# LSH attention with two feed-forward layers: first token block placed between the steps of the second batch's attention, one planned order for all engines, values unsplit, gate as one function

## Chip, cores and metric

One Trainium2 chip, one core. The time is the device time of one execution in microseconds (us), as a median over several runs. Engines: PE (TensorE: matmuls and transposes), DVE (VectorE), ACT (ScalarE), POOL (GpSimd), SP (issues DMAs).

## The reference, cut to what matters

```python
# q, k, v: (2 batches, 8 heads, 768 tokens, 64); proj: (64, 6); all matmul inputs f32 or f64
q_bucket = sum(((q @ proj) > 0) * powers); k_bucket = sum(((k @ proj) > 0) * powers)
scores = where(q_bucket[:, None] == k_bucket[None, :], q @ k.T / 8, -1e9)
attn = exp(scores - max); attn = attn / (sum(attn) + 1e-9)
x = (attn @ v) of all heads side by side             # (1536 tokens, 512)
h = x @ w_in                                         # (1536, 2048), w_in f64
x = (h * tanh(log1p(exp(min(h, 20))))) @ w_out       # (1536, 512)
out = (((x @ w1) * (x @ w2)) @ w3) @ w_out2          # widths 1024, 1024, 1024, 512
```

The f64 weights arrive as pairs of 32-bit words.

## The kernel before, in words

**Split numbers.** For f32 accuracy an operand is written as hi + lo, both in the format f32r, which the PE takes in one pass. A product is then three matmuls (`PASS`: hi·hi, hi·lo, lo·hi). A split is one ACT copy (hi) and one subtraction (lo) on DVE or POOL (`split`, L175 to 178).

**Weights.** A chunk of 128 x 1024 f64 numbers is loaded as 32-bit words (`load64`, 1 MB, L128), decoded to f32 by one ACT and three DVE passes (`decode_a`, `decode_b`: L136, L139, L162, L166), stored in DRAM as f32 for the two later token blocks (`keep`, L277), and split (L176, L177). There are 36 such chunks: 4 of `w_out2`, 8 of `w3`, 8 of `w_in`, 8 of `w_out`, 4 of `w1`, 4 of `w2`. The product `w3 @ w_out2` is made once (`wp_mm`, L806, 192 matmuls of 512 columns) and kept in DRAM as `wp`.

**Attention.** 16 heads of 6 row tiles are 96 steps. A step computes the scores of 128 queries against 768 keys (`scores`, four matmuls of 384 columns, L638), the maximum on DVE (L648), and the exponential with its sum on ACT (L652). Later each 128 x 384 piece of the exponentials is transposed on the PE (`t_step`, three transposes, L693), copied out as hi by ACT (L710) and lo by DVE (L711), and multiplied with the values (`av_step`, L729: two matmuls of 384 columns, one for hi and one for lo; V's hi and lo stand side by side in the 128 columns of the stationary operand). Each step has two such pieces. The four partial products of a head leave by ACT (L740) and go through DRAM (`x_d`, L745; row sums r through `r_d`; means of V through `mv_d`), because hi and lo halves and the two heads of a pair lie in different partitions. `x_split` (L351 to L365) reads them back and makes the split input of a token block. Before a head's scores, its queries and keys are split, transposed (`qk_transpose`, L560) and given bucket bits (`bits`, L590 to L615); the features and masks are moved between partitions by DMA (`qa<-qb`, `qa<-mk` and others).

**Feed-forward.** The 1536 tokens are three blocks of 512. A block is 672 matmuls of 512 columns: 192 for h (`h_mm`, L380), 192 for its output (`out_mm`, L1011), 192 for the two products with w1 and w2 (`ab_mm`, L1038), 96 for the last one (`o_mm`, L1062). The gate (`mish`, L414 to L424) is four DVE passes (one of them on POOL in some chunks) and three ACT functions (Exp, Ln, Exp) over 128 x 1024.

**Order.** `PLAN` at the top of the file says by hand at which attention step each piece of other work is traced (`tail`, `filler`, `prep`); Tile's scheduler orders by that. The attention runs alone with the weight product; of the first token block only three h chunks (72 matmuls) are traced among the last attention steps (`e0` to `e5`). The rest of the block follows the attention, then the second and third block (list `prog`). All DMAs but one are issued from SP. The lines of the hand-written order that the change removes are

```python
tl("xs", lambda: x_split(0))
tl("e0", lambda: h_early(0, 0, 0))
tl("m0", lambda: mish(0, 0))
segs = dict(s=seg_s, p=seg_p, n=seg_n, t=seg_t, f=seg_f, l=seg_l)
for c in PLAN["ord"]:
    segs[c]()
```

Of the kernel before, what the change touches and what calls it, by code (L numbers as in the profile page):

```python
# [8 lines left out]
PLAN = {'sp': [],  # L9
 'F32N': 0,  # L10
 'F32E': 1000,
 'GPM': [4, 5, 6],
 'GPL': [4],
 'wg': [2, 2, 2, 2],
 'kw': [0, 4, 0, 0, 0, 2],
 'pe1': 0,
 'ord': 'nsptlf',
 'sg': [203, 204],
 'bx': 1,
 'wo2n': [0, 3, 0, 3],  # L20
# [46 lines left out]
PSUM = bass.MemoryType.PSUM  # L67

# [4 lines left out]
DRAM = bass.MemoryType.DRAM  # L73
TINY = float(2.0 ** -80)
SIGN = -(2 ** 31)


@with_exitstack
def kernel(
# [22 lines left out]
    NP = NH // 2  # L102
# [3 lines left out]
    KR = D + 2 * NB  # L106

    const = ctx.enter_context(tc.tile_pool(name="const", bufs=1))
    big = ctx.enter_context(tc.tile_pool(name="big", bufs=2))
    strm = ctx.enter_context(tc.tile_pool(name="strm", bufs=2))  # L110
    ps = ctx.enter_context(tc.tile_pool(name="ps", bufs=1, space=PSUM))

    def ps_s(name, dt=F32):
        return ps.tile([128, 2, 512], dt, tag="s", name=name, bufs=2)

    dram = ctx.enter_context(tc.tile_pool(name="dram", bufs=1, space=DRAM))
    x_d = [dram.tile([DM, NT], F32, tag=f"x{i}", name=f"x_d{i}") for i in range(2)]
    r_d = dram.tile([2, DM // 128, NT], F32, tag="r", name="r_d")
    mv_d = [dram.tile([2, DM], F32, tag=f"mv{i}", name=f"mv_d{i}") for i in range(B)]
    wp_d = dram.tile([FF2, DM], F32, tag="wp", name="wp_d")  # L120
    ident = const.tile([128, 128], F32, tag="ident", name="ident")
    identr = const.tile([128, 128], FR, tag="identr", name="identr")

    c04 = const.tile([128, 1], F32, tag="c04", name="c04")

    def load64(src, n, pool=strm):
        raw = pool.tile([128, n, 1024 // n, 2], I32, tag="raw", name="raw", bufs=2)
        nc.sync.dma_start(out=raw.rearrange("p a b t -> p a (b t)"), in_=src)  # L128
        return raw, pool

    def decode_a(raw):
        raw, pool = raw
        n = raw.shape[1]
        g = pool.tile([128, n, 1024 // n], F32, tag="g", name="g", bufs=2)
        z = raw[:, :, :, 1]
        nc.scalar.activation(  # L136
            out=g, in_=raw[:, :, :, 1].bitcast(F32), func=AF.Copy, scale=2.0 ** -112
        )
        nc.vector.tensor_scalar(  # L139
            out=z, in0=g.bitcast(I32), scalar1=3, scalar2=None, op0=ALU.logical_shift_left  # L140
        )
        return raw, g, z

    def decode_b(state, sg=False):
        raw, g, z = state
        if sg:
            sg = min(sg, 2)
            nc.vector.scalar_tensor_tensor(
                out=z, in0=raw[:, :, :, 0], scalar=29, in1=z,
                op0=ALU.logical_shift_right, op1=ALU.bitwise_or,  # L150
            )
            if sg == 2:
                nc.gpsimd.tensor_scalar(
                    out=g, in0=g, scalar1=0.0, scalar2=2.0, op0=ALU.is_ge, op1=ALU.mult
                )
                nc.gpsimd.tensor_mul(out=g, in0=z.bitcast(F32), in1=g)
                nc.gpsimd.tensor_sub(out=g, in0=g, in1=z.bitcast(F32))
                return g
            nc.scalar.activation(out=g, in_=g, func=AF.Sign)
            nc.gpsimd.tensor_mul(out=g, in0=z.bitcast(F32), in1=g)  # L160
            return g
        nc.vector.scalar_tensor_tensor(  # L162
            out=z, in0=raw[:, :, :, 0], scalar=29, in1=z,
            op0=ALU.logical_shift_right, op1=ALU.bitwise_or,
        )
        nc.vector.scalar_tensor_tensor(  # L166
            out=g.bitcast(I32), in0=g.bitcast(I32), scalar=SIGN, in1=z,
            op0=ALU.bitwise_and, op1=ALU.bitwise_or,
        )
        return g  # L170

    def decode(raw, sg=False):
        return decode_b(decode_a(raw), sg)

    def split(src, n, hl, eng):  # L175
        nc.scalar.copy(out=hl[:, 0], in_=src)  # L176
        eng.tensor_sub(out=hl[:, 1], in0=src, in1=hl[:, 0])  # L177
        return hl

    PASS = ((0, 0), (0, 1), (1, 0))  # L180

    # ------------------------------------------------ loads of the feed-forward parts
    TB = 512
    NBK = NT // TB
    FP = FF // 256
    AP_ = FF2 // 256

    SB, HB = 2, 5
    late = []
    mid = []  # L190
    spare = []
    keep = {}
    chunks = {}
    order = []
    prog = []
    HL = PLAN["lookh"]
    for n in range(NBK):
        c = PLAN["cut"] if n + 1 < NBK else None
        nxt = []
        if c:  # L200
            for x in range(HL):
                nxt.append((c[x], [("h", n + 1, x), ("mish", n + 1, x), ("ms", n + 1, x)][:3 if x == 0 else 1]))

        def after(k):
            for kk, ops in nxt:
                if kk == k:
                    prog.extend(ops)

        for j in range(FP):
            if j + HL < FP and (n, j) != (0, 0):  # L210
                prog.append(("h", n, j + HL))
            elif n == 0 and j == 0:
                for x in range(3, HL + 1):
                    prog.append(("h", n, x))
            if j + 1 < FP:
                if (n, j) != (0, 0):
                    prog.append(("mish", n, j + 1))
                prog.append(("ms", n, j + 1))
            if n + 1 < NBK and j == (PLAN["xs1"] if n == 0 else PLAN["xs2"]):
                prog.append(("x", n + 1))  # L220
            prog.append(("out", n, j))
            after(j)
        prog.append(("x2", n))
        after(8)
        prog.append(("ab", n, 0))
        for f in range(FF2 // 128):
            if f + 1 < FF2 // 128:
                prog.append(("ab", n, f + 1))
            after(9 + f)
            prog.append(("o", n, f))  # L230
        after(17)
        prog.append(("fin", n))
    for j in range(3):
        order.append((0, "wi", j))
    order.append((0, "wo", 0))
    for op in prog:
        keys = {
            "h": lambda n, j: [(n, "wi", j)], "out": lambda n, j: [(n, "wo", j)],
            "ab": lambda n, f: [(n, "wa", f // 2), (n, "wb", f // 2)],
            "o": lambda n, f: [(n, "wp", f // 2)],  # L240
        }.get(op[0], lambda *a: [])(*op[1:])
        order.extend(x for x in keys if x not in order)
    issued = [0]

    loaded = {}
    decoded = {}
    nxt_ = [0, 0]

    def load_chunk(i):
        n, nm, j = order[i]  # L250
        pool = strm if i < 8 or i % 4 > 1 or nm in ("wa", "wb") else late[0]
        m = KD if nm in ("wi", "wa", "wb") else 2
        if n == 0 and nm != "wp":
            w = {"wi": w_in, "wo": w_out, "wa": w1, "wb": w2}[nm]
            if m == KD:
                src = w[:, j * 512:(j + 1) * 512].rearrange("(k p) f -> p k f", p=128)
            else:
                src = w[j * 256:(j + 1) * 256].rearrange("(f p) d -> p f d", p=128)
            loaded[i] = load64(src, m, pool)
        else:  # L260
            f = pool.tile([128, m, 1024 // m], F32, tag="g", name="f", bufs=2)
            if nm == "wp":
                nc.sync.dma_start(
                    out=f, in_=wp_d[j * 256:(j + 1) * 256].rearrange("(f p) d -> p f d", p=128)
                )
            else:
                nc.sync.dma_start(out=f.rearrange("p a b -> p (a b)"), in_=keep[nm, j])
            loaded[i] = f

    def decode_chunk(i):  # L270
        n, nm, j = order[i]
        f = loaded.pop(i)
        if n == 0 and nm != "wp":
# [7 lines left out]
    def load_to(i):  # L281
        while nxt_[0] < min(i, len(order)):
            load_chunk(nxt_[0])
            nxt_[0] += 1
# [344 lines left out]
    E = {}  # L629
# [512 lines left out]
```

## Time and profile before

| what | value |
|---|---|
| median of 3 runs | 942.21 us (939.95 to 947.37) |
| span of the profiled execution | 967.6 us |
| PE busy | 822.8 us, 85% of the span |
| DVE busy | 667.6 us, 69% |
| ACT busy | 512.5 us, 53% |
| POOL busy | 203.4 us, 21% |
| DMA | 125.99 MB, 69545 packets, 23152 of them under 512 B |

The profiled execution is one execution of its own; its span is 25.4 us above the median of the runs. PE's busy time is a union of intervals that include each matmul's latency, so a price of a matmul is better read from the distance of two starts than from its duration.

### The profile page before, as it was taken

How to read it: one execution, taken by the hardware profiler on the slowest of the kernel's cores; microseconds unless marked ns; L12 is line 12 of the kernel's file. 1: busy time of each engine (PE TensorE's matmuls, PEld its weight loads, DVE VectorE, ACT ScalarE, POOL GpSimd, SP SyncE). 2: the span in 40 equal slices, each digit the busy share in tenths (PEclk: the TensorE clock that was granted, in tenths of full speed). 3: DMA queues.
4: the chain of work that ended last, by engine and by line, in shares of the span. 5: the costliest groups of instructions: out<-in, count | busy, mean ns of one | idle time of the engine just before them, and what ended most of it. 6: DMA issues, size and time to landing. Idle time of an engine off the chain costs nothing. (4 is left out here: it accounts for less than half of the span.)

```text
span 967.6 us, 11292 instructions
## 1 busy us (share of the span) xinstructions
PE 822.8 (85%) x3923; PEld 686.2 (71%) x3923; DVE 667.6 (69%) x823; ACT 512.5 (53%) x801; POOL 203.4 (21%) x219
## 2 busy tenths in 40 slices
PE   7767987867889666889767398989999999999998
PEld 6656876756777656767545276768888888888886
DVE  6866865754878657877879999975775744766422
ACT  3745774644658364775555456335664633665321
POOL 3240320130203113122275743440000000000000
PEclk8799899988999797989979698989999999999999
DMA  6686798665596855648764566644233233332101
GB/s 203 182 147 134 126 145 152 121 128 102 125 101 83 179 79 111 104 118 100 249 233 159 168 217 214 220 152 150 89 95 102 88 87 108 131 109 88 44 22 44
DMA packets 69545, 125.99 MB, mean 130 GB/s; under 512 B 23152, under 2 KB 33648, under 8 KB 68464
## 3 DMA queue, kind: packets, MB, share of 16 engines
q1 hardware_dynamic: 69344, 125.14, 54.0%
q8 instruction: 31, 0.51, 0.2%
q14 instruction: 26, 0.21, 0.1%
q10 hardware_dynamic: 144, 0.13, 0.0%
HBM read 88.09 MB, written 24.17 MB: 116 GB/s over the span
## 5 line engine op out<-in xcount | busy, mean ns | idle before, releaser
L1011 PE MATMUL x2a<-ghl,hl 128*128 128x512 f32 x552 | 135.9, 403 | 33.3 <-ACT ghl L430 20.4
L1011 PEld LDWEIGHTS x2a<-ghl,hl 128*128 128x128 f32 x552 | 106.4, 194 | 60.6 <-ACT ghl L430 22.2
L729 PE MATMUL pv<-ethl,hlv 128*128 128x384 f32 (+1 forms) x384 | 131.5, 410 | 13.7 <-POOL ethl L709 10.1
L380 PE MATMUL hps<-xhl,hl 128*128 128x512 f32 x552 | 138.4, 401 | 3.9 <-POOL hl L177 3.9
L710 ACT CAST ethl<-et 128x384 fp32r<-128x384 f32 x192 | 90.9, 483 | 92.6 <-PE et L693 83.0
L1038 PE MATMUL abp<-x2hl,hl 128*128 128x512 f32 x576 | 137.2, 394 | 0.0
L711 DVE TENSOR_TENSOR ethl<-et,ethl 128x384 fp32r<-128x384 f32 x192 | 102.9, 551 | 38.9 <-ACT ethl L710 36.9
L1038 PEld LDWEIGHTS abp<-x2hl,hl 128*128 128x128 f32 x576 | 108.1, 188 | 25.8
L380 PEld LDWEIGHTS hps<-xhl,hl 128*128 128x128 f32 x552 | 106.0, 193 | 27.7 <-POOL hl L177 4.3
L693 PE MATMUL et<-ident,E 128*128 128x128 f32 x576 | 106.8, 295 | 21.4 <-DVE ethl L711 21.1
L648 DVE TENSOR_REDUCE st<-ts 128x1 f32<-128x768 f32 x96 | 91.1, 949 | 30.0 <-PE ts L638 29.4
L693 PEld LDWEIGHTS et<-ident,E 128*128 128x128 f32 x576 | 78.4, 152 | 36.2 <-DVE ethl L711 26.8
L652 ACT ACTIVATE E<-ts,st 128x768 f32<-128x768 f32 x96 | 87.4, 911 | 15.3 <-DVE st L648 14.0
L177 DVE TENSOR_TENSOR hl<-f,hl 128x1024 fp32r<-128x1024 f32 x56 | 71.9, 1283 | 32.4 <-ACT hl L176 32.3
L1062 PE MATMUL oac<-hl,phl 128*128 128x512 f32 x288 | 77.2, 420 | 10.3 <-ACT phl L1049 7.1
L729 PEld LDWEIGHTS pv<-ethl,hlv 128*128 128x128 f32 x384 | 68.2, 209 | 18.4 <-POOL ethl L709 10.9
L1062 PEld LDWEIGHTS oac<-hl,phl 128*128 128x128 f32 x288 | 57.9, 203 | 26.3 <-ACT phl L1049 7.9
L638 PE MATMUL ts<-ka,qa 76*128 76x384 f32 x192 | 58.6, 386 | 21.0 <-DMA qa<-mk 12.4
L176 ACT CAST hl<-f 128x1024 fp32r<-128x1024 f32 x60 | 62.9, 1048 | 25.6 <-PE x2a L1011 12.1
L177 POOL TENSOR_TENSOR hl<-g,hl 128x1024 fp32r<-128x1024 f32 x17 | 55.5, 3264 | 61.9 <-ACT hl L176 61.8
L162 DVE SCALAR_TENSOR_TENSOR raw<-raw 128x1024 int32<-128x1024 int32 x34 | 62.0, 1824 | 0.3
L638 PEld LDWEIGHTS ts<-ka,qa 76*128 76x128 f32 x192 | 38.7, 215 | 29.5 <-DMA qa<-mk 10.3
(120 smaller groups left out, 1193.7 us busy)
## 6 DMA issues: line engine op xcount, KB each, us to landing
raw<-in_moe_w_dram SPq DMA_DIRECT2D x16, 1024.0 KB
raw<-in_moe_w_out_dram SPq DMA_DIRECT2D x12, 1024.0 KB
raw<-in_moe_w_in_dram SPq DMA_DIRECT2D x8, 1024.0 KB
f<-keep_wi SPq DMA_DIRECT2D x16, 512.0 KB
f<-keep_wo SPq DMA_DIRECT2D x16, 512.0 KB
x_d<-ptmp SPq DMA_DIRECT2D x64, 96.0 KB
xi<-x_d SPq DMA_DIRECT2D x24, 256.0 KB
f<-wp_d SPq DMA_DIRECT2D x12, 512.0 KB
```

The lines of the kernel that those rows point to most:

```text
L177: eng.tensor_sub(out=hl[:, 1], in0=src, in1=hl[:, 0])
L380: nc.tensor.matmul(o, lhsT=w[:, ws, kk, f * 128:(f + 1) * 128], rhs=xh[xs][:, kk, :], start=(m == 0), stop=(m == 3 * KD - 1),)
L638: nc.tensor.matmul(t[:, a, 0:HS], lhsT=l[0:kk, i * 128:(i + 1) * 128], rhs=r[0:kk, a * HS:(a + 1) * HS], start=(l is qa), stop=(l is qb),)
L648: nc.vector.tensor_reduce(out=s[:, 0, i:i + 1], in_=t[:, :, 0:HS], axis=AX.XY, op=ALU.max, negate=True)
L652: nc.scalar.activation(out=e.rearrange("p (a n) -> p a n", a=2), in_=t[:, :, 0:HS], func=AF.Exp, bias=s[:, 0, i:i + 1], accum_out=s[:, 1, ...
L693: nc.tensor.transpose(t[:, ci * 128:(ci + 1) * 128], E[u, a * CH + ci][:, kt * 128:(kt + 1) * 128], ident,)
L710: nc.scalar.copy(out=hl[:, 0, 0:HS], in_=t[:, 0:HS])
L711: nc.vector.tensor_sub(out=hl[:, 1, 0:HS], in0=t[:, 0:HS], in1=hl[:, 0, 0:HS])
L729: nc.tensor.matmul(t[:, 0:n], lhsT=vhl_t[u][:, kt].rearrange("p s d -> p (s d)"), rhs=hl[:, s, 0:n], start=(kt == 0 and j == 0), stop=(las ...
L1011: nc.tensor.matmul(x2a[n][d], lhsT=w[:, ws, f, d * 128:(d + 1) * 128], rhs=g[:, gs, f, :], start=(j == 0 and f == 0 and s == 0), stop=(j = ...
L1038: nc.tensor.matmul(t[:, i, :], lhsT=ws_[i][:, ws, kk, (f % 2) * 128:(f % 2) * 128 + 128], rhs=xh[:, xs, kk, :], start=(m == 0), stop=(m == ...
L1062: nc.tensor.matmul(oac[n][t], lhsT=g[:, gs, t * 128:(t + 1) * 128], rhs=w[:, ws, f % 2, :], start=(f == 0 and s == 0), stop=(f == FF2 // 1 ...
```

## The change

The file is rewritten around a planner. Every operation becomes a unit with an engine (or a choice of ACT and DVE), a cost, buffers it reads and writes, and a due time in attention steps. `Plan.run` simulates the six queues, takes on each the ready unit with the earliest due time, assigns buffers, and then traces all units in the order of their planned starts, with Tile's own reordering off (`manual_schedule`).

```diff
-PLAN = {'sp': [],
...
+CFG = {
+    "lag": 1.0,
...
+    "dec0": 35.0,
+    "dec1": 78.0,
+    "ff0": 48.5,
+    "ff1": 103.0,
...
+class Plan:
+    LAT = {"PE": 0.22, "DVE": 0.17, "ACT": 0.17, "POOL": 0.3, "SP": 2.3, "SWAP": 0.0}
...
+            u.start, u.eng = s, e
...
+        order.sort(key=lambda u: (u.start, u.idx))
+        for u in order:
+            u.fn(u.eng) if len(u.alts) > 1 else u.fn()
...
+    ctx.enter_context(tc.manual_schedule())
...
-        nc.scalar.copy(out=hl[:, 0, 0:HS], in_=t[:, 0:HS])
-        nc.vector.tensor_sub(out=hl[:, 1, 0:HS], in0=t[:, 0:HS], in1=hl[:, 0, 0:HS])
...
+        def cp(eng):
+            (nc.scalar.copy if eng == "ACT" else nc.vector.tensor_copy)(out=f()[:, 0:HS], in_=t()[:, 0:HS])
...
+    def values(u, a, j, due):
...
+            for x in range(2):
+                nc.tensor.matmul(
+                    t()[x * D:(x + 1) * D, 0:n], lhsT=vs[u]()[:, 2 * j + x, :], rhs=fs[x]()[:, 0:n],
+                    start=(j == 0), stop=(j == CH - 1))
+        P.op("PE", 0.67, mm, r=fs + [vs[u]], w=[t], due=due, name=f"V{u}.{a}.{j}")
...
+                nc.vector.tensor_add(
+                    out=xv[rows, kk, c - blk * TB:c1 - blk * TB], in0=t()[0:D, c - n0:c1 - n0], in1=tm()[:, c - n0:c1 - n0])
...
+        P.op("POOL", 1.0, lambda: nc.gpsimd.dma_start(
+            out=raw().rearrange("p (m n) -> p m n", m=m), in_=src), w=[raw], due=due, lat=8.0, name=nm + "l", after=after)
...
-        nc.scalar.activation(out=e, in_=e, func=AF.Exp)
-        nc.vector.scalar_tensor_tensor(out=t, in0=e, scalar=2.0, in1=e, op0=ALU.add, op1=ALU.mult)
-        nc.scalar.activation(out=e, in_=t, func=AF.Ln, scale=0.2, bias=c04[:, 0:1])
-        nc.scalar.activation(out=e, in_=e, func=AF.Exp, scale=-1.0)
...
+            P.op("ACT", act(1024, True) + 2.7, lambda: nc.scalar.activation(out=hs(), in_=hs(), func=AF.Mish),
+                 r=[hs], w=[hs], due=dm, name=f"mish{G}")
...
+        h_group(0)
+        h_group(1)
+        for G in range(NG):
+            if G + 2 < NG:
+                h_group(G + 2)
+            x2_group(G)
...
+    x_split(0, H * C + 0.5, [x for x in P.units if x.name == f"wp{GT - 1}.0"])
+    ff_first(0, CFG["ff0"], CFG["ff1"])
```

What moves where:

- Values and exponentials stay f32 and unsplit: 192 f32 matmuls of 384 columns (64 output partitions each, two key tiles side by side in the upper and lower half of the PSUM tile) take the place of 384 f32r ones. Each transposed piece is copied once, by ACT or DVE. The halves are added (ACT copy, DVE add) straight into X in SBUF; `x_d` and `mv_d` are gone, and the row sums go to DRAM as rows after a PE transpose.
- The first block (`ff_first`) is spread over steps 48.5 to 103, that is over the second batch's attention and a little beyond. It accumulates in PSUM only within a chunk and adds the chunks up in SBUF (`x2a`, `oa`: 64 DVE passes of 512), and it fetches its 28 weight chunks from the kept f32 copies.
- The gate is ACT's function Mish. In the first block it stands between the attention's Exp, which belongs to another table of ACT.
- POOL computes nothing after the setup. Its low halves, products and splits go to DVE; POOL issues the 36 loads of f64 words (two buffers of them) and the stores of the decoded chunks.
- Masks and features are copied between partitions by DVE or ACT, except `xf`, which stays a DMA.
- The second and third block keep their matmuls and their two-deep PSUM, with Mish read directly from PSUM.

## Rows read from the trace of the kernel before

**Rows 1.** The page's first part: span, and busy time of the engines.

```profile
span 967.6 us, 11292 instructions
PE 822.8 (85%) x3923; PEld 686.2 (71%) x3923; DVE 667.6 (69%) x823; ACT 512.5 (53%) x801; POOL 203.4 (21%) x219
```

**Rows 2.** Stretches: PE, PEld, DVE, ACT, POOL busy (count); clock; DMA share; GB/s.

```profile
16.00:450.00 434.00, 344.94 (x1927) 302.96 (x1927) 306.55 (x476) 257.14 (x512) 94.85 (x158) 0.89 0.70 126
450.00:640.00 190.00, 142.41 (x552) 110.21 (x550) 174.31 (x137) 96.59 (x106) 100.98 (x38) 0.87 0.63 203
640.00:967.00 327.00, 323.71 (x1392) 262.66 (x1392) 177.06 (x179) 153.97 (x177) 2.39 (x1) 0.99 0.28 92
```

**Rows 3.** The chain that ended last: start us, length us, what.

```profile
639.35 0.63 ACT phl L1049
...
640.02 5.71 PE oac L1062 x12
...
676.33 5.50 PE x2a L1011 x24
...
964.17 0.42 DVE mh L1075
```

**Rows 4.** PE's timeline, 0 to 42 and 130 to 140: start, length, engine, line.

```profile
16.05 0.84 PE L638 MATMUL ts<-ka,qa 76*128 76x384 f32 x2
...
27.70 0.71 PE L560 MATMUL tqk<-identr,hlq 128*128 128x128 f32 x6
...
130.04 0.52 PE L693 MATMUL et<-ident,E 128*128 128x128 f32 x3
130.31 0.60 PE L729 MATMUL pv<-ethl,hlv 128*128 128x386 f32 x2
130.75 0.49 PE L693 MATMUL et<-ident,E 128*128 128x128 f32 x3
...
133.82 0.86 PE L806 MATMUL wacc<-wo,w3t 128*128 128x512 f32 x3
134.52 0.52 PE L638 MATMUL ts<-ka,qa 76*128 76x384 f32 x2
134.87 0.51 PE L638 MATMUL ts<-kb,qb 128*128 128x384 f32 x2
```

**Rows 5.** DVE: its timeline, 525 to 560; tile raw (min/median/max ns); groups by line.

```profile
524.20 3.44 DVE L166 SCALAR_TENSOR_TENSOR g<-g,raw 128x1024 int32<-128x1024 int32 x1
...
537.09 1.21 DVE L166 SCALAR_TENSOR_TENSOR g<-g,raw 128x1024 int32<-128x1024 int32 x1
...
L139 DVE TENSOR_SCALAR raw<-g x36: 678/693/2882, 29.3 to 623.6; 128x1024 int32<-128x1024 int32 x36
L162 DVE SCALAR_TENSOR_TENSOR raw<-raw x34: 1209/1226/3423, 30.6 to 624.3; 128x1024 int32<-128x1024 int32 x34
...
L711 DVE TENSOR_TENSOR ethl<-et,ethl 128x384 fp32r<-128x384 f32 x192 | 102.9, 551 | 38.9 <-ACT ethl L710 36.9 <-DVE ethl L711 0.9
L648 DVE TENSOR_REDUCE st<-ts 128x1 f32<-128x768 f32 x96 | 91.1, 949 | 30.0 <-PE ts L638 29.4
L1024 DVE TENSOR_TENSOR x2hl<-x2a,x2hl 128x512 fp32r<-128x512 f32 x12 | 8.2, 687 | 3.7 <-ACT x2hl L1023 3.6
```

**Rows 6.** ACT's groups by line: count | busy us, mean ns | idle before.

```profile
L652 ACT ACTIVATE E<-ts,st 128x768 f32<-128x768 f32 x96 | 87.4, 911 | 15.3 <-DVE st L648 14.0
...
L652 ACT ACTIVATION_READ_ACCUMULATOR E<-ts,st 128x1 f32 x96 | 19.7, 206 | 0.0
...
L441 ACT ACT_TABLE_LOAD x1 | 1.3, 1283 | 0.7 <-PEq L1123 0.7
```

**Rows 7.** One f64 chunk, 440 to 480: its issue on SP, its first use on ACT.

```profile
447.00 0.74 SPq L128 DMA_DIRECT2D raw<-in_moe_w_in_dram  x1
...
465.13 1.12 ACT L136 ACTIVATE g<-raw 128x1024 f32<-128x1024 f32 x1 [6.90 <-DMA raw<-in_moe_w_in_dram]
...
472.54 1.05 ACT L176 CAST hl<-g 128x1024 fp32r<-128x1024 f32 x1 [3.48 <-DVE g L166]
```

More of the change, by code (lines that the diff above doesn't have):

```diff
@@ L67 @@
 PSUM = bass.MemoryType.PSUM
+DRAM = bass.MemoryType.DRAM
 BIG = float(2.0 ** 30)
@@ L118 @@
[L118 to L129, printed above, removed]
@@ L172, in decode @@
[L172 to L180, printed above, removed]
     TB = 512
     NBK = NT // TB
+    GT = FF2 // 128
     FP = FF // 256
[L186 to L191, printed above, removed]
-    keep = {}
[L193 to L196, printed above, removed]
@@ L233 @@
[L233 to L247, printed above, removed]
@@ L249, in load_chunk @@
[L249 to L268, printed above, removed]
@@ L1088, in o_step @@
[L1088 to L1105 removed]
+    ctx.enter_context(tc.manual_schedule())
+    P = Plan()
@@ new lines, with warm @@
+    ccol = ctile([128, 2], "ccol")
+    prow = ctile([128, NB], "prow")
+    pq = ctile([128, 2, 2, NB], "pq", FR)
+    mvs = ctile([128, B * KD], "mvs")
+    nc.scalar.preload_act_table_set("exp_and_others")
+    make_identity(nc, ident)
+    nc.vector.memset(zr.bitcast(F32), 0.0)
+    nc.scalar.copy(out=identr, in_=ident)
+    v_id, v_psel, v_psel2, v_ccol = Val(), Val(), Val(), Val()
+    NWARM = CFG["warm"]
+    def warm():
+        t = SP_.bufs[1]
+        for _ in range(NWARM):
+            nc.tensor.matmul(t[:, 0, 0:128], lhsT=zr, rhs=zr, start=True, stop=True)
@@ new lines, with copy, load_head, go @@
+    EITHER = ("ACT", "DVE")
+    def copy(e, o, i):
+        (nc.scalar.copy if e == "ACT" else nc.vector.tensor_copy)(out=o, in_=i)
+    raws, hls, feat, xfs, vs = {}, {}, {}, {}, {}
+    def load_head(u, due, after=()):
+        b, h = divmod(u, H)
+        for nm, src in (("q", q), ("k", k)):
+            t = raws[u, nm] = Val(RW, "r")
+            def go(t=t, src=src):
+                nc.sync.dma_start(out=t(), in_=src[b, h].rearrange("(p c) d -> p c d", c=C))
+            P.op("SP", 0.5, go, w=[t], due=due, name=f"load{nm}{u}", after=after)
@@ new lines, in decode_chunk @@
+    def decode_chunk(nm, j, due, waits=None):
+        raw = rawload(chunk_src(nm, j), due - 1.5, f"{nm}{j}", after=late_gate + (waits or []))
+        g = Val(F4, "g", 2)
+        decode(raw, g, due, f"{nm}{j}")
+        keep[nm, j] = dram.tile([128, 1024], F32, tag=f"{nm}{j}", name=f"keep_{nm}{j}")
+        kept[nm, j] = Val()
+        P.op("POOL", 1.0, lambda: nc.gpsimd.dma_start(out=keep[nm, j], in_=g()), r=[g], w=[kept[nm, j]],
+             due=due + 0.4, lat=4.5, name=f"{nm}{j}s")
+    hl_lim, ld_lim, fx_lim, late, fetched = [CFG["hl"]], [2], [1], [""], []
@@ new lines, in split, with wview @@
+    def split(f, hl, due):
+        P.op("ACT", act(1024, True), lambda: nc.scalar.copy(out=hl()[:, 0:1024], in_=f()),
+             r=[f], w=[(hl, 0)], due=due, name="hi")
+        P.op("DVE", dve(1024), lambda: nc.vector.tensor_sub(
+            out=hl()[:, 1024:2048], in0=f(), in1=hl()[:, 0:1024]), r=[f, (hl, 0)],
+            w=[(hl, 1)], due=due + 0.1, name="lo")
+    def wview(hl, m):
+        return hl().rearrange("p (s a b) -> p s a b", s=2, a=m)
+    wo2 = [Val(K8, "big", 4, FR) for _ in range(GT // 2)]
@@ new lines @@
+    warm()
+    load_head(0, -20)
+    setup()
+    load_v(0, -7)
+    load_head(1, -6)
+    load_v(1, -5)
+    NS = NH * C
+    early_gate, late_gate = [], []
+    prep(0, -8, 1)
+    early_gate.append(P.units[-1])
+    for u in range(NH):
+        n0 = u * C
+        if u + 2 < NH:
+            load_head(u + 2, n0 + 0.5)
+            load_v(u + 2, n0 + 1.5)
+        if u + 1 < NH:
+            prep(u + 1, n0 + C - CFG["prep"] + 0.35, (CFG["prep"] - 0.6) / 5.0)
+        for i in range(C):
+            scores(u, i, n0 + i)
+            if u == 0 and i == 0:
+                late_gate.append(P.units[-1])
+        for a in range(2):
+            d0 = n0 + a * CH + CH - 1 + CFG["lag"]
+            for kt in range(C):
+                unit(u, a, kt, d0 + kt * 0.5)
+                if kt % 2:
+                    values(u, a, kt // 2, d0 + kt * 0.5 + 0.6)
+        norm(u, n0 + C)
@@ new lines @@
+    for i in range(GT // 2):
+        wo2_chunk(i, CFG["wp0"] - 4 + i)
+    per = (CFG["wp1"] - CFG["wp0"]) / GT
+    for f in range(GT):
+        wprod(f, CFG["wp0"] + per * f, CFG["wp0"] + per * (f + 1))
+    seq = []
+    for j in range(FP):
+        seq.append(("wi", j))
+        if j % 2 and j > 1:
+            seq += [("wo", j - 3), ("wo", j - 2)]
+    seq += [("wo", FP - 2), ("wo", FP - 1)]
+    for j in range(GT // 2):
+        seq += [("wa", j), ("wb", j)]
+    for x, (nm, j) in enumerate(seq):
+        decode_chunk(nm, j, CFG["dec0"] + (CFG["dec1"] - CFG["dec0"]) * x / len(seq))
@@ new lines, with step_list, after @@
+    hl_lim[0], ld_lim[0], fx_lim[0], late[0] = 7, 3, 2, "2"
+    first0 = fetched[-1]
+    seqs = []
+    def step_list():
+        prog = []
+        HLK = 3
+        cut = [7, 7, 15]
+        for n in range(1, NBK):
+            nxt = []
+            if n + 1 < NBK:
+                for x in range(HLK):
+                    nxt.append((cut[x], [("h", n + 1, x)]))
+            def after(k):
+                for kk, ops in nxt:
+                    if kk == k:
+                        prog.extend(ops)
+            if n == 1:
+                for x in range(HLK):
+                    prog.append(("h", n, x))
+            for j in range(FP):
+                if j + HLK < FP:
+                    prog.append(("h", n, j + HLK))
+                if n + 1 < NBK and j == 5:
+                    prog.append(("x", n + 1))
+                prog.append(("out", n, j))
+                after(j)
+            prog.append(("x2", n))
+            after(8)
+            prog.append(("ab", n, 0))
+            for f in range(GT):
+                if f + 1 < GT:
+                    prog.append(("ab", n, f + 1))
+                after(9 + f)
+                prog.append(("o", n, f))
+            after(17)
+        return prog
@@ new lines, in b_x2 @@
+    def b_x2(n):
+        d = clock[0]
+        xs2 = x2h[n] = [Val(K8, "big", 6, FR) for _ in range(2)]
+        for dd in range(KD):
+            t = xa[n][dd]
+            xx = xs2[dd // 2]
+            P.op("ACT", act(512), lambda t=t, xx=xx, dd=dd: nc.scalar.copy(out=kview(xx, 0, dd), in_=t()), r=[t], w=[(xx, (0, dd))],
+                 due=d - 20, name="x2h")
+            P.op("DVE", dve(512), lambda t=t, xx=xx, dd=dd: nc.vector.tensor_sub(out=kview(xx, 1, dd), in0=t(), in1=kview(xx, 0, dd)),
+                 r=[t, (xx, (0, dd))], w=[(xx, (1, dd))], due=d - 20, name="x2l")
@@ L1106 @@
+    x_split(1, 98)
+    OPS = {"h": b_h, "out": b_out, "x2": b_x2, "ab": b_ab, "o": b_o, "x": lambda n: x_split(n, clock[0] - 10, [P.units[-1]])}
+    for op, *a in step_list():
         OPS[op](*a)
-        if op == "ms" and a == [0, 1]:
-            ahead(0, "wi", 1)
+    global LAST
+    LAST = P.run()
 _INS = ['q', 'k', 'v', 'proj', 'moe_w_in', 'moe_w_out', 'moe2_w1', 'moe2_w2', 'moe2_w3', 'moe2_w_out']
```

1635 lines of the change are left out of this document (765 added, 870 removed).

## The prediction, made before the change was run

> **What bounds the kernel now.** I read the page's first part, then busy time by stretches, then the chain that ended last, then the timelines of PE, DVE and ACT for prices.
>
> The first part says only that PE is busiest [rows 1]; an average over stages doesn't tell what a stage is worth. The stretches [rows 2] show three regimes. From 640 on PE is busy 323.7 of 327.0 us: nothing but fewer matmuls can shorten that. From 450 to 640 DVE is busy 174.3 of 190 and POOL 101; PE does 552 matmuls, at 0.23 us each 127 us of work, so it is two thirds used. From 16 to 450, the attention, no engine is full: PE 345 of 434 by intervals (less by prices, below), DVE 307, ACT 257.
>
> The chain [rows 3] agrees: from 640.02 to the end it is PE without a break, whereas at 639.35 it still runs through ACT. Counting back, blocks two and three are 2 x 672 = 1344 of the 1392 matmuls after 640. So the first block ends some 11 us after 640, and the time to win is in the 650 us before that.
>
> Why is DVE full there? The same decode pass takes 1.21 us at 537.09 and 3.44 us at 524.20 [rows 5]; POOL is at work over half of that stretch [rows 2]. I read this as DVE held up by POOL, and part of the fullness as waiting.
>
> **PE prices**, from distances of starts [rows 4]: four score matmuls 0.70 us (134.52 to 134.87 is 0.35 for two); three transposes 0.26 (130.04 to 130.31 is 0.27); three matmuls of 512 columns 0.70. For the dense stretch I take 0.231 each, between 5.50 / 24 = 0.229 [rows 3] and 323.7 / 1392 = 0.233 [rows 2]. Two split value matmuls cost 0.44 (130.31 to 130.75).
>
> **The change, part by part, on PE.** Let A be the time at which the first block is done and only blocks two and three are left.
>
> Per step: scores 0.70; two transposed pieces 0.52; one values unit. Before, a step's values were four f32r matmuls, 0.88. The trace has no unsplit f32 matmul. An f32 product of the same accuracy holds four partial products, as hi and lo spelled out; if the two halves of the unit run side by side in the array, that is four times a pass of 384 columns, 4 x 0.175 = 0.70. Below: two plain passes, 0.35. Above: four passes each, one half after the other, 1.40. I take 0.70, next to 0.88 for as many partial products. Preparing a head: 12 transposes (six 0.54, the 0.71 of the row less the 0.17 by which neighbours overlap) 1.08, and six bit matmuls 1.05, together 0.36 per step. A step is thus 2.28 us, 96 steps 219 us.
>
> The weight product is 192 x 0.233 + 64 transposes x 0.087 = 50 us, unchanged. The first block is 672 x 0.231 = 155 us, unchanged in number, but moved beside the second batch's steps. PE before A: 219 + 50 + 155 = 424 us.
>
> Before, the stretch 16 to 450 held about the same 219 + 16 (values at 0.88) + 50 and 72 early matmuls (17): some 302 of 434, a use of 0.70. The stretch 450 to 640 used PE at 0.67. The gain can only come from a better use.
>
> **On DVE**, with its prices undisturbed by POOL [rows 5]: 96 maxima x 0.949 = 91; 36 decodes x (0.693 + 1.226 + 1.21) = 113; 40 low halves of 1024 (28 fetched chunks, 8 gates, 4 of w_out2) x 1.21 = 48; about 108 passes of 512 (64 chunk sums, x2, the w1/w2 products, w3, the first two token blocks' input) x 0.69 = 75; per head two splits, mask, copy and the adding of halves, about 3.9, times 16 = 62; normalisation 8. Sum 397. Gone are 192 subtractions for the exponentials (102.9), four gate passes per chunk, and the waits on POOL. Against it stand what POOL did and the 64 sums.
>
> **On ACT** [rows 6]: 96 x (0.911 + 0.206) = 107; 36 decodes at 1.12 [rows 7] = 40; 40 copies of 1024 at 1.05 [rows 7] = 42; some 68 copies of 512 at 0.63 [rows 3] = 43; features 32 x 0.82 = 26 and value halves 32 x 0.5 = 16 (both estimated between those); 8 Mish at 1.05 plus a table load there and back, 2 x 1.283, = 29. Sum 303. Gone are Ln and two Exp per chunk and the 192 forced hi copies.
>
> Left are some 250 copies that either may do (192 transposed pieces at 0.5, the rest smaller), 125 us. Spread evenly, DVE and ACT come to (397 + 303 + 125) / 2 = 413 us each, just under PE's 424. So a gate pass saved or a table load added is hidden as long as PE stays ahead, and if PE's share fell, these two would be late next at 413. POOL's moved work is paid in that sum.
>
> **DMA.** The way of x through DRAM goes (64 writes of 96 KB and 24 reads of 256 KB), and so do the mask copies on which scores waited. The 36 f64 loads move from SP to POOL's queue, the only other thing there being the 24 stores. The fetches of kept weights stay on SP, where in the second batch they now stand among the loads of heads and the `xf` copies. I cost these at nothing: the cover is the two-buffer lead of each; without it, see the fourth rival.
>
> **The use of the three engines.** With loads of 424, 413 and 413 in fixed orders, none can be full. The trace gives two bounds: 0.70 as in the attention before, and 174.3 / 190 = 0.92, DVE where it was the bound. I take 0.85, nearer to the upper: the waits that made 0.70 (masks by DMA, POOL between DVE operations) go, and first-block matmuls stand ready wherever a score waits for its maximum.
>
> **Sum.** The first score came at 16.05 [rows 4]; the change prepares one head before it, not two, so 13. A = 13 + 424 / 0.85 = 512. Blocks two and three 1344 x 0.231 = 310, with the same PE-bound order. After the last matmul some 4 us, as before (its end lies just under 964.17 [rows 3], the span is 967.6). Span 512 + 310 + 4 = 826. The profiled span before is 967.6 for a median of 942.2; in proportion 826 becomes 804, with the same 25.4 us off 801. Predicted: 803.
>
> **The rivals.**
>
> *Values in series* (14%). The two halves wait for each other: unit 1.40, PE + 67 = 491. PE is then clear of the others and I let it reach 0.90: A = 13 + 546 = 559, span 873, time 850. For it: two half-width matmuls side by side occur nowhere in this trace. Against it: nothing in a row.
>
> *Each values unit empties the array* (8%). A matmul's result is complete 0.17 us after the next could start [rows 4]. If the array must be empty before and after a pair, a unit costs 0.34 more, 33 us in all; PE 457 at 0.88, A = 532, span 846, time 824. The Trainium skill, "TensorEngine Tiling (Array Packing)", section "Key Properties", says that tiles work independently but that changing the tiling mode drains the engine. By its first half the pair is side by side, by its second this rival holds; no row here shows either.
>
> *The order stays the bound* (10%). Planned starts don't come true, engines wait for each other in fixed queues, and use stays at 0.70: A = 13 + 606 = 619, span 933, time 908. For it: before, too, first-block matmuls lay among attention steps at the end and PE was not full. Against it: 0.92 where one queue had work enough.
>
> *Slower: f64 chunks late* (4%). All 36 go through two buffers, so the last is decoded after 18 turns. One turn seen: issue 447.00, first use 465.13, decoded by 472.54 [rows 7], 25.5 us. At that rate the loads alone end at 15 + 18 x 25.5 = 474, 20 us of matmuls follow, and A = 512 hides it, narrowly. Slower by 1% needs a span of 977, A = 663, a turn of 35 us. Decisive is thus whether loads in POOL's queue take 10 us longer than the worst seen; without the many packets under 512 B they should be faster. The Trainium skill, "SBUF — State Buffer", section "SBUF: two separate sides", warns that a DMA issued from POOL has its descriptors written by POOL, which DVE's two-port copies lock out. The kernel before issues none there, so no row shows it; rows 5 show the reverse, DVE held by POOL.
>
> *The rest* (2%): no change within 1%.
>
> **Chances and range.** The likeliest case, 803, has 62%; its own range runs from use 0.92 (A = 474, span 788, less 25.4: 762) to use 0.80 (A = 543, span 857, 835). Values in series at 0.87 give span 891, 868. I take 762 to 870, which leaves out the order-bound and the slow case and values at 0.35 (PE 390, near 745). About 1% is what a measurement of this kernel can tell from no change. Every case but the last two is faster by more: 0.94; same 0.02; slower 0.04.
>
> **What would show it.** Right: PE busy without gaps between 250 and the end of the first block, with h and x2 matmuls among scores; scores of 96 steps done near 490; DVE passes of 1024 at 1.21 throughout; two value matmuls starting within a few ns of each other, the next operation about 0.7 later; the last 1344 matmuls in 310 us. Wrong: the second half of a values pair starting 0.6 late; PE idle until ACT or DVE in the second batch; decodes waiting for raw chunks; the first block's matmuls piled up after the last score. The sum falls first with the use of 0.85, which is a judgement between two rows; each 0.01 is 6 us.

## The result, and the profile after

The changed kernel takes 845.45 us (median of 4 runs, 845.2 to 846.31), 0.897 of the kernel before, with an interval of 0.892 to 0.902. Forecast were 803 us and a range of 762 to 870: the direction and the range hold, the number is 42 us too low. 845 lies next to the forecast of a rival (values in series, 850), but that rival is not the cause, as the second experiment shows.

The page's first part after, to be held against [rows 1]:

```profile
span 843.4 us, 10408 instructions
PE 804.5 (95%) x3938; PEld 607.6 (72%) x3938; DVE 553.6 (66%) x784; ACT 464.2 (55%) x731; POOL 42.1 (5%) x84
```

PE is busy for nearly as long as before (804.5 us against 822.8), the other engines for less. Busy time by stretches, columns as in [rows 2], divided where the first block ends:

```profile
13.00:514.00 501.00, 480.29 (x2550) 347.99 (x2550) 423.48 (x632) 349.19 (x593) 34.61 (x53) 0.97 0.50 169
514.00:840.00 326.00, 314.24 (x1345) 250.90 (x1343) 122.83 (x132) 109.55 (x131) 0.00 (x0) 1.00 0.27 92
```

The first row takes the place of the first two of [rows 2]: 501 us in place of 624 (plus the start), PE near full and DVE at 85%, the clock granted at 0.97 in place of 0.89 and 0.87. The second row is the surprise: 1345 matmuls take 326 us, almost the 327 that 1392 took before. The chain (start us, length us, what) says where the first block ends and what happens later:

```profile
34.03 5.93 DMA xf<-kb
...
212.20 9.36 DMA f<-r_d
...
300.41 9.86 DMA keep_wo<-f
...
502.97 11.15 PE b L748 x48
514.12 21.77 PE s L732 x96
...
834.00 5.55 PE b L1146 x24
```

L748 is the first block's last product, L732 the second block's h: A, the end of the first block, is 514.1 us. Three DMAs stand in the chain before it, 25 us in all: a copy of features, a read of row sums and the store of a decoded chunk. L1146 is the last product of block three. Inside block two, in a closer view of the chain:

```profile
613.31 3.48 PE s L1118 x15
616.79 0.02 issue
616.81 0.59 ACT f L1126
617.41 0.04 issue
617.45 5.83 PE s L1118 x24
```

Here PE stops after 15 of the 24 matmuls of the products with w1 and w2 until ACT has copied the first product out of PSUM (L1126). The row of that group gives the sum of these waits, 11.3 us; they are 16, each 0.7 us:

```profile
L1118 PE MATMUL s<-k,k 128*128 128x512 f32 x384 | 95.4, 398 | 11.3 <-ACT f L1126 11.3
```

In the kernel before the same group (L1038) waited for nothing and lay in the chain in whole pieces of 24.

DVE after (min/median/max ns of one), to be held against the last of the decode passes in [rows 5], which took 1.21 or 3.44 us:

```profile
L572 DVE SCALAR_TENSOR_TENSOR f<-f,k x36: 1183/1218/1394, 26.0 to 386.1; 128x1024 int32<-128x1024 int32 x36
```

With POOL computing nothing, none of the 36 takes longer than 1.4 us.

The unsplit values, PE's timeline in two windows, the first of 0.1 us (a row holds all matmuls of one line that touch the window):

```profile
126.91 0.54 PE L526 MATMUL b<-T,v 128*64 128x384 f32 x2
...
126.91 0.87 PE L526 MATMUL b<-T,v 128*64 128x384 f32 x4
127.70 0.88 PE L506 MATMUL b<-ident,E 128*128 128x128 f32 x6
128.34 0.59 PE L463 MATMUL s<-kb,qb 128*128 128x384 f32 x2
```

A unit's two f32 matmuls appear as four records. Two are under way in the first window; together they last 0.54 us, as long as one lasts alone (0.537), so they start within 10 ns of each other. The next work starts at 127.70: the unit costs 0.79 us. Six transposes cost 128.34 - 127.70 = 0.64, that is 0.107 each where six follow each other.

### The profile page after: what moved, and what is told of

Its sections match the earlier page's. It is cut to its first block, busy times and chain, and to the rows that moved or that the text cites. A ratio compares the mean times of both kernels' runs of the same rounds, so it can differ in the third digit from the quotient of the medians.

```text
span 843.4 us, 10408 instructions
## 1 busy us (share of the span) xinstructions
PE 804.5 (95%) x3938; PEld 607.6 (72%) x3938; DVE 553.6 (66%) x784; ACT 464.2 (55%) x731; POOL 42.1 (5%) x84
## 2 busy tenths in 40 slices
DMA packets 40354, 118.44 MB, mean 140 GB/s; under 512 B 4496, under 2 KB 10992, under 8 KB 39280
## 4 chain that ended last, share of the span: by engine, by line
PE 86%; DVE 5%; ACT 3%; DMA 3%; issue 2%; POOL 0%; SPq 0%; DVEq 0%; ACTq 0%; POOLq 0%
PE s L1118 11%; PE b L1091 11%; PE s L732 10%; PE b L526 8%; PE b L748 8%; PE b L506 7%; PE s L463 7%; PE b L843 6%; PE b L1146 5%; PE b L668 5%; PE b L732 5%; PE s L436 2%; PE s L405 1%; DMA keep_wo<-f 1%; ACT f L1126 1%
## 5 line engine op out<-in xcount | busy, mean ns | idle before, releaser
L620 DVE TENSOR_TENSOR k<-f,k 128x1024 fp32r<-128x1024 f32 x96 | 116.5, 1220 | 101.4 <-ACT k L618 101.3
L618 ACT CAST k<-f 128x1024 fp32r<-128x1024 f32 x96 | 99.5, 1047 | 14.8 <-DMA f<-keep_wi 9.2
L1118 PE MATMUL s<-k,k 128*128 128x512 f32 x384 | 95.4, 398 | 11.3 <-ACT f L1126 11.3
L506 PE MATMUL b<-ident,E 128*128 128x128 f32 x576 | 96.6, 280 | 4.5 <-ACT E L475 2.9
L475 ACT ACTIVATE E<-s,st 128x768 f32<-128x768 f32 x96 | 86.6, 903 | 23.7 <-DVE st L472 23.2
L472 DVE TENSOR_REDUCE st<-s 128x1 f32<-128x768 f32 x96 | 91.1, 951 | 12.9 <-PE s L463 11.7
L1118 PEld LDWEIGHTS s<-k,k 128*128 128x128 f32 x384 | 70.9, 188 | 33.6 <-ACT f L1126 18.2
L1091 PE MATMUL b<-k,k 128*128 128x512 f32 x384 | 90.3, 393 | 0.0
L732 PE MATMUL s<-k,k 128*128 128x512 f32 x384 | 89.9, 391 | 0.0
L526 PE MATMUL b<-T,v 128*64 128x386 f32 (+1 forms) x384 | 84.6, 519 | 0.0
L1091 PEld LDWEIGHTS b<-k,k 128*128 128x128 f32 x384 | 72.1, 188 | 16.5
L732 PEld LDWEIGHTS s<-k,k 128*128 128x128 f32 x384 | 72.1, 188 | 15.9
L748 PE MATMUL b<-k,k 128*128 128x512 f32 x288 | 78.6, 407 | 0.3 <-DVE k L808 0.3
L748 PEld LDWEIGHTS b<-k,k 128*128 128x128 f32 x288 | 50.8, 188 | 21.3 <-issue 9.0
L732 PE MATMUL b<-k,k 128*128 128x512 f32 x192 | 54.3, 416 | 7.7 <-ACT k L717 5.0
L668 PE MATMUL b<-k,k 128*128 128x512 f32 x192 | 55.9, 411 | 0.0
L843 PE MATMUL b<-k,k 128*128 128x512 f32 x192 | 54.1, 411 | 0.0
```

The source lines that it names most:

```text
L472: P.op("DVE", 0.868, lambda: nc.vector.tensor_reduce(out=s()[:, 0, i:i + 1], in_=t()[:, :, 0:HS], axis=AX.XY, op=ALU.max, negate=True), r= ...
L506: nc.tensor.transpose(t()[:, ci * 128:(ci + 1) * 128], es[ci]()[:, kt * 128:(kt + 1) * 128], ident)
L526: nc.tensor.matmul(t()[x * D:(x + 1) * D, 0:n], lhsT=vs[u]()[:, 2 * j + x, :], rhs=fs[x]()[:, 0:n], start=(j == 0), stop=(j == CH - 1))
L618: P.op("ACT", act(1024, True), lambda: nc.scalar.copy(out=hl()[:, 0:1024], in_=f()), r=[f], w=[(hl, 0)], due=due, name="hi")
L620: P.op("DVE", dve(1024), lambda: nc.vector.tensor_sub(out=hl()[:, 1024:2048], in0=f(), in1=hl()[:, 0:1024]), r=[f, (hl, 0)], w=[(hl, 1)], ...
L668: nc.tensor.matmul(acc(), lhsT=hv()[:, ws, g_, :], rhs=wview(wo2[g_ // 2], 2)[:, rs, g_ % 2, :], start=(n == 0), stop=(n == 3 * GT - 1))
```

## The experiments

The times of variants are compared with the 845.45 us of the changed kernel, or, from the eighth on, with that of the first experiment. Experiments 2 to 7 are single runs, the others four.

The variants ran in three groups, on three chips: 1 to 4, 5 to 8, 9 and 10. The kernel before, run beside each group, had medians of 963.5, 940.4 and 942.8 us, so ratios to it can't be compared between groups, and the changed kernel itself was not run again. What can be compared is the stretch that most variants leave alone: blocks two and three take 325.4 us in the changed kernel and 324.9 to 325.9 in experiments 2, 3, 5, 6 and 7, on two of these chips. The end of the first block is less firm: experiment 1 changes nothing before it, yet planned anew it ends 2.3 us later. A difference of 3 us may thus be the order alone.

**1. The copy behind both products.**

```diff
-    r=[(t, 0)], w=[p], due=d + 12, name="pa")
+    r=[t], w=[p], due=d + 24, name="pa")
```

> Blocks two and three: the copy of the first of the two products (w1) out of PSUM is put behind both products, not between them, as in the kernel before. Theory: in the changed kernel PE stands 0.7 us in front of the second product, 16 times, because the copy reads the tile that PE goes on writing (11.3 us in the waits of the changed kernel); without it the stretch after 514 us shrinks from 325 to 312 us and the time from 845.5 to 832 to 835 us. Rival: PE is held by the buffers behind the copy, and the wait comes back in another place; then the time stays above 842 us.

Measured 832.9 us (831.56 to 835.81); ratio to the kernel before 0.868, interval 0.862 to 0.873. The chain's pieces are whole again, and the first and the last of them show the stretch:

```profile
516.41 21.77 PE s L732 x96
...
629.53 5.48 PE s L1118 x24
...
820.98 5.58 PE b L1146 x24
```

From 516.41 to 826.56 it is 310.1 us, against 514.1 to 839.6, 325.4, in the changed kernel. The theory holds: 15 us were lost by where a copy stands among matmuls. The time falls by 12.6, since the first block ends 2.3 us later. That the wait comes from tracking the PSUM tile as a whole, though the copy reads one bank and PE writes the other, is my reading of it; shown is that it goes when the copy moves.

**2. Both value matmuls on the same 64 partitions.**

```diff
-    t()[x * D:(x + 1) * D, 0:n], lhsT=vs[u]()[:, 2 * j + x, :], rhs=fs[x]()[:, 0:n],
-    start=(j == 0), stop=(j == CH - 1))
+    t()[0:D, 0:n], lhsT=vs[u]()[:, 2 * j + x, :], rhs=fs[x]()[:, 0:n],
+    start=(j == 0 and x == 0), stop=(j == CH - 1 and x == 1))
```

> Both value matmuls of a unit go to the same 64 PSUM partitions, one after the other, and the adding of two halves (a copy on ACT, an add on DVE) becomes one copy; the plan is told 1.34 us for a unit. Theory: the two halves ran side by side, so a unit grows from 0.80 us to about 1.5 us, 96 x 0.7 = 67 us more of PE, and as PE is the bound of the first 514 us the time goes to 890 to 915 us. Rival, the halves took turns anyway: unit stays near 0.8 us, time 835 to 848 us.

Measured 888.9 us, just under the theory's range. A unit in this kernel's timeline, and the chain where the second block begins:

```profile
128.79 1.50 PE L526 MATMUL b<-T,v 128*64 128x384 f32 x4
130.22 0.50 PE L665 MATMUL b<-k,k 128*128 128x512 f32 x1
```

```profile
557.70 21.77 PE s L729 x96
```

1.43 us from start to start, against 0.79: the halves of the changed kernel do run side by side. 96 x 0.64 = 61 us more of PE move the end of the first block from 514 to 557.7, by 43.6; the rest PE took from its gaps (busy 536 of 544 us there) and from a granted clock of 0.99 in place of 0.97. Values in series is not what happened, and PE's work does count in this stage.

**3. The first block behind the attention.**

```diff
-    x_split(0, H * C + 0.5, [x for x in P.units if x.name == f"wp{GT - 1}.0"])
+    x_split(0, H * C + 0.5, [x for x in P.units if x.name == f"S{NH - 1}.{C - 1}"])
```

> The input of the first token block is made only after the last score has been issued, so its 672 matmuls follow the attention; all else is as in the changed kernel, planned anew. Theory: the second batch's attention has 125 us of PE work, but needs 150 (its DVE load) to 205 us (48 steps at the 4.28 us of the kernel before), and the block then costs 155 / 0.92 = 169 us, so the first block is done at 530 to 590 instead of 514 us: time 870 to 920 us. Rival, putting the block between the steps is worth nothing, since DVE's work sets both: time within 8 us of 845.

Measured 875.2 us. Busy time of the second batch's scores and of the block behind them, and the chain where the second block begins:

```profile
210.00:367.00 157.00, 137.19 (x776) 89.78 (x775) 141.76 (x220) 121.77 (x240) 21.13 (x31) 0.96 0.61 202
367.00:543.00 176.00, 166.15 (x722) 130.80 (x721) 108.05 (x141) 78.25 (x103) 0.00 (x0) 0.98 0.34 108
```

```profile
543.69 21.82 PE s L732 x96
```

Alone the second batch fills DVE most (142 of 157, PE 137), the block fills PE; one after the other they end at 543.7, together at 514.1. Interleaving is worth 30 us, less than a third of the 99 us gained. The attention itself became quicker: 157 us for these 48 steps is 3.3 us a step, and the first 48, with the weight product among them, take 197 us (4.1), where 96 steps took 411 us (4.3) in the kernel before.

**4. Split values.**

```diff
-    (nc.scalar.copy if eng == "ACT" else nc.vector.tensor_copy)(out=f()[:, 0:HS], in_=t()[:, 0:HS])
+    nc.scalar.copy(out=f()[:, 0, 0:HS], in_=t()[:, 0:HS])
...
+    nc.vector.tensor_sub(out=f()[:, 1, 0:HS], in0=t()[:, 0:HS], in1=f()[:, 0, 0:HS])
...
+    t()[:, 0:m], lhsT=vs[u]()[:, kt].rearrange("p s d -> p (s d)"), rhs=fs[x]()[:, s, 0:m],
```

> Undoes the unsplit values alone: V and the transposed exponentials are split again (ACT copies all 192 pieces, DVE subtracts 192 times), a unit is four matmuls of 384 columns in one pass each; one of 12 large buffers is given up for the room. Theory of three engines with like loads: DVE gets 192 x 0.55 us less the 75 copies it did (41), so 65 us more, ACT 36 us more, and both become later than PE: first block done 20 to 50 us later, time 865 to 895 us. Rival, PE alone sets the first 514 us and split units (0.70 to 0.88 us against 0.80) are no dearer: time 835 to 850 us.

Measured 891.1 us, within the theory's range. The stretch to the end of the first block, and the group that was added:

```profile
13.00:560.00 547.00, 483.02 (x2553) 406.93 (x2554) 489.59 (x785) 390.04 (x685) 33.74 (x53) 0.94 0.48 160
```

```profile
L519 DVE TENSOR_TENSOR T<-b,T 128x384 fp32r<-128x384 f32 x192 | 104.7, 551 | 15.5 <-ACT T L517 14.3
```

DVE's busy time in the stretch grows from 423 to 490 us and the stretch from 501 to 547, with PE's busy time unchanged (483 against 480). ACT's grows too, from 349 to 390, the granted clock falls from 0.97 to 0.94, and the room holds one large buffer fewer and four transposed pieces in place of seven. So the 46 us are those of splitting with all that it needs; DVE's share alone is not shown.

**5. The gate of the first block in three functions and four passes.**

```diff
-    lambda: nc.scalar.activation(out=hs(), in_=hs(), func=AF.Mish),
+    lambda: nc.scalar.activation(out=ge(), in_=ge(), func=AF.Exp),
...
+    lambda: nc.scalar.activation(out=ge(), in_=gt(), func=AF.Ln, scale=0.2, bias=c04[:, 0:1]),
```

> Undoes the gate of the first block alone: three functions on ACT (Exp, Ln, Exp, all in one table set with the attention's Exp) and four passes on DVE in place of Mish; blocks two and three keep Mish. The 14 table loads go. DVE gets 8 x (0.7 + 3 x 1.21) = 35 us more, ACT 8 x 2 x 1.05 = 17 us more and 14 x 1.28 = 18 us less. Theory of three engines with like loads: DVE, already 413 us of 514, becomes the latest and the time grows by 12 to 30 us, 857 to 875 us. Rival, PE alone sets the first 514 us: within 5 us of 845.

Measured 875.5 us, at the upper end of the theory's range. The first block ends at 544.9, 31 us later, for 29 us more of DVE (165.75 + 286.58 = 452 in these rows, 423 before). The rows, and the chain where the second block begins:

```profile
13.00:200.00 187.00, 175.82 (x996) 126.94 (x997) 165.75 (x249) 132.66 (x244) 11.03 (x17) 0.97 0.53 175
200.00:546.00 346.00, 316.39 (x1561) 229.26 (x1562) 286.58 (x407) 218.71 (x363) 24.11 (x36) 0.96 0.45 151
```

```profile
544.86 21.77 PE s L734 x96
```

One for one, although DVE is busy 85% only. The longer chain of a gate and its buffers may have a part; that was not tried apart.

**6. A function that needs no table load.**

```diff
-    lambda: nc.scalar.activation(out=hs(), in_=hs(), func=AF.Mish),
+    lambda: nc.scalar.activation(out=hs(), in_=hs(), func=AF.Tanh),
```

> The first block computes tanh(h) instead of the gate (the table in use for the attention's Exp has it, so no table is loaded there); it leaves the gate's function out of that block. ACT has 14 x 1.28 = 18 us less work and exponentials are no longer held 3.6 us behind a gate. Theory: hidden, as PE is the bound: 840 to 846 us. Rival, ACT's order bounds the second batch: 825 to 835 us.

Measured 844.6 us: hidden. ACT's busy time falls from 349 to 332 us, and A is 513.4 in place of 514.1:

```profile
13.00:514.00 501.00, 480.58 (x2553) 349.33 (x2553) 424.51 (x631) 332.43 (x581) 34.81 (x53) 0.98 0.51 169
```

In the changed kernel the loads are

```profile
L781 ACT ACT_TABLE_LOAD x7 | 9.0, 1283 | 0.1
L475 ACT ACT_TABLE_LOAD x7 | 9.0, 1283 | 0.1
```

(L781 is Mish, L475 the attention's Exp.)

**7. The f64 chunks on SP's queue.**

```diff
-    P.op("POOL", 1.0, lambda: nc.gpsimd.dma_start(
+    P.op("SP", 0.5, lambda: nc.sync.dma_start(
```

> The 36 loads of f64 chunks and the 24 stores of decoded ones are issued from SP, not from POOL. Theory: the queue does not matter, loads are ahead of their use: 840 to 852 us. Rival 1, DVE's copies hold up the issue on POOL: 5 us or more faster. Rival 2, on SP they stand before the short loads of heads, masks and row sums: 10 us or more slower.

Measured 842.3 us, 3 us less, within the theory's range and no more than another order may make: the queue hardly matters. The page's issue rows of the changed kernel (last column: median us to landing) show why no chunk was late:

```profile
k<-in_moe_w_dram POOLq DMA_DIRECT2D x16, 1024.0 KB, 7.8
k<-in_moe_w_out_dram POOLq DMA_DIRECT2D x12, 1024.0 KB, 8.9
...
k<-in_moe_w_in_dram POOLq DMA_DIRECT2D x8, 1024.0 KB, 7.3
```

They landed in 7 to 9 us. The page before gives no such median; the one chunk of [rows 7], for which ACT waited, was first used 18 us after its issue. There are fewer small packets now (4496 under 512 B, 23152 before) and fewer bytes; whether either made the transfers quicker was not tried.

**8. Two DMA waits.** On top of experiment 1:

```diff
-    P.op("SP", 0.5, lambda sl=sl, fb=fb: nc.sync.dma_start(
-        out=xf()[sl].bitcast(F32), in_=fb()[sl].bitcast(F32)), r=[fb], w=[(xf, nm)], due=d(2.5), lat=2.0, name=f"xf{u}")
+    P.op(EITHER, (act(S, True), dve2(S)), lambda e, sl=sl, fb=fb: copy(e, xf()[sl], fb()[sl]),
+         r=[fb], w=[(xf, nm)], due=d(2.5), name=f"xf{u}")
...
-    due=due, lat=2.3,
+    due=due, lat=9.0,
```

> On top of the copy put behind both products: the key and query features for the bits are copied by ACT or DVE, not by DMA, and the plan is told 9 us (not 2.3) for the reads of the row sums and 4 us (not 2.2) for their writes. Theory: PE's two longest stands in the first 514 us were waits for DMAs that were planned at 2.0 and 2.3 us and took 5.9 us (features, at 34) and 9.4 us (row sums, at 212), and 8 to 12 us of them come back: 821 to 826 us. Rival: other work was short there too and the time stays at 830 to 835 us.

Measured 828.0 us (824.03 to 829.25), 5 us less than experiment 1, between the two forecasts. The block ends at 511.0 in place of 516.4, and no DMA is left in the chain:

```profile
511.01 21.93 PE s L732 x96
```

So the two waits, 15 us as they stand in the changed kernel's chain, were worth at most a third of that, and 2 to 3 us of it may be the order planned anew. The rest of that time was bound by other work.

**9. Values units in groups.** On top of experiment 1:

```diff
-                if kt % 2:
-                    values(u, a, kt // 2, d0 + kt * 0.5 + 0.6)
+                if kt in (3, 5):
+                    values(u, a, (0, 1) if kt == 3 else (2,), d0 + kt * 0.5 + 0.6)
```

> On top of the copy put behind both products: of the three values units of a head's half the first two are issued together, so 64 groups of side-by-side matmuls in place of 96. Theory: around each group PE loses about 0.2 us (0.09 before its first matmul, 0.04 and 0.06 behind it, by starts in the changed kernel) in changing between half-width and full-width matmuls, 32 changes fewer give 6 us: 825 to 829 us. Rival: these gaps are weight loads that any neighbour would show, nothing is gained or the longer groups hold scores up: 831 to 838 us.

Measured 822.3 us (821.69 to 823.72), 10.6 us less than experiment 1 and more than expected; ratio to the kernel before 0.883, interval 0.869 to 0.897. That interval is wide, and the verdict against the kernel before unclear, with the latter's runs beside it between 925 and 959 us. A double unit, and the chain where the second block begins:

```profile
130.35 1.52 PE L528 MATMUL b<-T,v 128*64 128x386 f32 x8
131.80 0.96 PE L670 MATMUL b<-k,k 128*128 128x512 f32 x3
```

```profile
506.86 21.77 PE s L734 x96
```

1.45 us for two, against 0.79 or 0.80 for one: the second costs 0.65, so 0.15 of a single unit is the price of entering and leaving. With the 0.09 in front that the expectation counted, 32 groups fewer account for 8 us, and the first block ends 9.6 us earlier than in experiment 1; the rest I put down to a different order. Whether the price belongs to the half width or to the f32 format is open: the full-width f32r units of experiment 4 start 0.17 us behind the last score matmul, like any follower, where these start 0.27 behind it, but there both differ.

**10. All three together.**

> All three together: copy behind both products, features copied by ACT or DVE and longer row-sum times in the plan, values units grouped. If the gains add (5 us measured for the second, 6 expected for the third): 820 to 824 us. If PE's order is the bound in another place: 826 to 830 us.

Measured 827.5 us (827.21 to 828.85): the gains don't add. Experiment 9 remains the fastest, 2.7% under the changed kernel. The loss against experiment 9, run beside it, lies ahead of the second block, which begins at 510.9 in place of 506.9 us; blocks two and three take 310 us in both. Which wait in that stage costs it is open.

## Why the prediction was right, and where its 42 us went

*From the profile to the runs: wrong, 23 us.* The step "in proportion 826 becomes 804", with 803 at its end, failed. The profiled execution of the kernel before was simply longer than its runs (967.6 against 940 to 950 us). The span of an execution is not longer than its time: in every run of the record it is some 1.8 us shorter (843.4 for 845.22). A span of 967.6 fits the runs of the same kernel beside experiments 1 to 4, 955 to 973 us. Without the step the forecast is 826 to 828.

*Blocks two and three, "1344 x 0.231 = 310, with the same PE-bound order": wrong, 15 us.* The price was right, experiment 1 gives 310.1. The order was not the same: the diff traces the first product's copy between the matmuls of the second, and I read "keep their matmuls" as if it said all. The other 4 us are A, 2 us late, and 2 from the span to the median.

*A = 512: right, 514.1, but by luck, as two errors cancel.* PE's work was mis-sized. A values unit costs 0.80 and 0.09 in front of it, not 0.70; a transpose 0.107 to 0.109 where they stand in sequence, not 0.087. A step is thus 0.70 + 0.65 + 0.89 + 0.36 = 2.60, not 2.28, and PE's sum 250 + 50 + 155 = 455, not 424. Against that the use of PE is 455 / 501 = 0.91, not 0.85; the upper of my two bounds, 0.92, was the nearer. What the sum leaves out is PE's clock. By the rows, its mean grant was 0.89 and 0.87 before and 0.97 after; with its two levels of 1.2 and 2.4 GHz that is some 144 us at the lower one before, 30 after. In the changed kernel PE was busy 1.0 of 5 us behind the wait for row sums (220 to 225), and in the next 5 us the clock was 0.50. A lone values unit at 0.50 takes 1.49 us, not 0.80. Part of the better use is thus a better clock; how much was not measured apart.

*Three engines with like loads: right for PE and DVE, not for ACT.* DVE measured 423 us of 501 (forecast 413), ACT 349 (forecast 413; of the 192 copies it took 117). Experiments 2, 4 and 5 add 61 us to PE, 66 and 29 to DVE (the fourth 41 to ACT as well), and the stage grows by 44, 46 and 31. Experiment 6 takes 17 us from ACT and nothing moves.

*"A gate pass saved is hidden as long as PE stays ahead": wrong.* I read this as PE being ahead of DVE by too little to hide 29 us. The gate as one function in the first block is worth about 30 us, the unsplit values about 46, the interleaving about 30, each measured by one run without it. That they sum to 106 is no account of the 99 won: these are net of the 15 lost in blocks two and three, the parts share two engines, and POOL at rest, X kept in SBUF and the planned order itself were not undone alone.

*DVE held up by POOL: borne out by the 36 decode passes* at 1.18 to 1.39 us, and by the trace before. There 22 decode passes took over 1.4 us, all of them while POOL was computing, and the 54 passes with POOL idle took at most 1.23; the excess is 35 us of DVE. It is an agreement of two traces, not an experiment: POOL's work was not put back alone.

*The rivals.* Values in series fell with experiment 2. The array emptied around each unit is half right: 0.24 us a unit (0.15 and 0.09), against 0.34 as forecast and none in my likeliest case. The Trainium skill, "TensorEngine Tiling (Array Packing)", section "Key Properties", on draining at a change of tiling mode: the traces agree in kind, with 0.80 for a lone unit and 0.65 for one that follows another. The order as the bound fell: 0.91. Late f64 chunks fell, with landings of 7 to 9 us and experiment 7; the Trainium skill's warning on DMAs issued from POOL ("SBUF — State Buffer", section "SBUF: two separate sides") is at most the 3 us of that run here. A slip in the range: values at 0.35 (PE 390) give by the same sum a span of 786 and 761 to 765 us, not 745, at the edge of the range and not clear of it.

## What to carry to other kernels

When an order is planned by a model, look in the profile for waits that the model doesn't know; here a copy planned between two halves of one PSUM tile cost 15 us in the one stage that looked untouched. Ask of a saved DVE pass not whether DVE is the busiest engine but how far ahead the busiest is: at 91% for PE and 85% for DVE, a microsecond on either cost 0.7 to 1. And take the factor from profile to runs as 1: compare a span with the time of the same execution, not with the median of others.

## What the runs showed of the hardware

An f32 matmul of 384 columns with 64 output partitions appears as two records, 0.32 to 0.37 us from start to start. A lone pair of them side by side costs 0.80 us, one after the other 1.43; a pair that follows another side by side costs 0.65. "FP8 and Floating Point Precision" of the Trainium skill, section "TensorE Precision Notes", counts four passes for true f32. The traces agree roughly: each of the two records is about as long as two f32r matmuls of 384 columns, 0.35 us in [rows 4].

Changing from full-width f32r matmuls and transposes to half-width f32 ones and back cost some 0.24 us (0.15 by experiment 9 and 0.09 in front), unseen in PE's busy time (25.00 of 25.00 us in many stretches).

A table load took 1.28 us and the next function started right behind it; leaving out the 14 of them between exponentials, with Tanh in place of Mish, changed the time by 1 us in the one run of experiment 6.
